# Sums over features split between the two row halves of TensorE, with an order of matmuls and banks laid out by a plan

## The chip, the cores and the metric

The kernel runs on one core of a Trainium2 chip. The metric is the device time of one execution in microseconds (us). The engines are TensorE (PE, matmuls; PEld its weight loads), VectorE (DVE), ScalarE (ACT), GpSimd (POOL) and SyncE (SP), which here issues most DMAs.

## The reference

One attention block and one gated feed-forward block read the same normalised rows; their results are multiplied and added to the input. S = 2048 rows, D = 576 features, 32 heads of 18, F = 4608 hidden features, all float32.

```python
xn = layernorm(x)
q, k, v = split_heads(xn @ wqkv)                    # 32 heads of 18
p = softmax(q @ k.T * 18 ** -0.5)
s = merge_heads(p @ v) @ wo
gate, up = xn @ W_gate, xn @ W_up                   # 576 -> 4608
h = gate * (gate > 0) * up
g = silu(h @ W_down)                                # 4608 -> 576
out = x + s * g
```

## The kernel before

Each float32 operand of a large product is split into a high part (float32r) and a remainder, and a product is the sum of three matmuls (`PRODUCTS`: high x high, high x rest, rest x high). The products of probabilities and values (`po`) are plain float32.

**Row halves.** TensorE's array is used as two tiles of 64 rows and 128 columns, which work at the same time on two different sums. D = 576 is nine chunks of 64 features (`KC`). Each tile of x holds one such chunk twice, on partitions 0 to 63 and on 64 to 127; gate weights lie on the lower half, up weights on the upper one. `row_half` gives the 27 matmuls of one sum (9 chunks x 3 products) on one half, and `row_pairs` deals them out in turn for the two halves. Maxima of scores (`pm`, reduced by DVE at L189) and scores for the exponentials (`psx`, evicted by ACT at L624) also take 64 rows each: head 0 of a pair on the lower half, head 1 on the upper one.

**Projections.** For each of four groups of 512 rows: layer norm, nine transposes (`tps`) with a split by ACT and DVE, four blocks of q and k (`pq`) with a rest block `qk_last` every second group, then v (`pv`). q, k and v go to DRAM. In the last group the first heads' k and q strips are loaded (`load_k`, `load_q`, DMAs at L147) behind block 0 of four.

**Units.** There are 144 units: 36 blocks of 128 hidden features for each 512 rows. `emit_unit` writes the order of PE by hand: 27 steps of `up` on each half (`pg`), mixed at even distances with maxima (`max_steps`, for the next pair of heads) and scores (`exp_steps`). After it `attend` multiplies the four tiles of probabilities that are ready by the values (`po`, tiles of 128 rows and 32 columns, added up in one bank `psO` over four units), and after every second unit `down` runs 48 matmuls of `py` on the whole array, then `run_tasks` does what was put off: a transpose of the maxima (`tp`, its rows written into qT by eight DMAs from `nt`, L572) and the normalisation of a finished output. The first 16 units (`N1`) have maxima only; then each of the 16 pairs of heads has 8 units (`UN`).

**Other engines.** POOL splits the gate and up weights (`gw`), the down weights (`dw`) and the hidden tile (`hh`). DVE adds `py` to the sums `ys` (L503). When 512 rows are complete, their gate value (silu) is made in small pieces between the units (`gate_steps`: exponential on ACT, reciprocals on DVE at L524) and stored in DRAM. At the end the output projection (`pw`) runs for 16 tiles of 128 rows, multiplied by the gate and added to x.

PSUM has eight banks: five shared by `pm`, `psx`, `py` and transposes, one for `po`, two for `pg`. PE's instructions keep the order of the program.

## Time and profile before

| | |
|---|---|
| median of 3 runs | 2690.13 us (2689.19 to 2692.2) |
| the profiled execution | span 2689.7 us, 0.4 us below that median; no other time of its own is given |
| mean granted TensorE clock | 0.998 |
| PE busy | 2664.5 us (99%) |
| DVE, ACT, POOL busy | 1904.3, 1386.8, 1249.1 us (71%, 52%, 46%) |
| DMA | 248.68 MB, 92 GB/s on average |

Where a row is a group, it gives line, engine, operation, output and inputs, shapes and count, then the busy time in us and the mean of one in ns, then idle time before it and what ended it. Rows of the chain or of a timeline begin with start and length in us. Busy times of overlapping matmuls are counted once for the group and in full for the mean.

### The profile page before, as it was taken

What the parts mean: (1) busy time and instruction counts of PE and PEld (TensorE: products, weight loads), DVE (VectorE), ACT (ScalarE), POOL (GpSimd) and SP (SyncE); (2) the same over time, 40 slices, a digit from 0 to 9 for tenths busy, and PEclk for the clock granted to TensorE, in tenths of its full rate; (3) what the DMA queues carried; (4) which work ended last, traced back from release to release, by engine and by line L of the source; (5) the groups of instructions that cost most, each with busy time, mean ns of one, the idle gap of its engine ahead of it and who ended that gap; (6) DMA issues with size and microseconds to landing.
All of it is one profiled execution on the core that took longest, in us unless ns stands there. A gap on an engine that the chain in (4) does not pass through costs nothing.

```text
span 2689.7 us, 55016 instructions
## 1 busy us (share of the span) xinstructions
PE 2664.5 (99%) x22092; PEld 2084.7 (78%) x22092; DVE 1904.3 (71%) x3252; ACT 1386.8 (52%) x2566; POOL 1249.1 (46%) x1021
## 2 busy tenths in 40 slices
PE   7999999999999999999999999999999999999999
PEld 6998987777777787777777777777777777777778
DVE  5426667777777777777777877777777787776135
ACT  3321125555565555555566555555555555555551
POOL 5226664444444444444444454444445444444543
PEclk9999999999999999999999999999999999999999
DMA  9745332222532322232353222222252322222237
GB/s 241 221 158 140 93 76 68 65 70 73 121 97 61 83 64 74 61 77 63 76 128 86 71 75 64 74 69 67 73 122 78 85 76 70 70 64 56 57 102 229
DMA packets 289471, 248.68 MB, mean 92 GB/s; under 512 B 60416, under 2 KB 232192, under 8 KB 289216
## 3 DMA queue, kind: packets, MB, share of 16 engines
q1 hardware_dynamic: 281152, 216.85, 32.1%
q0 software_dynamic: 8064, 28.32, 3.1%
q8 instruction: 174, 2.85, 0.5%
q14 instruction: 81, 0.66, 0.1%
HBM read 199.74 MB, written 44.83 MB: 91 GB/s over the span
## 4 chain that ended last, share of the span: by engine, by line
PE 95%; DMA 2%; DVE 1%; POOL 1%; issue 1%; SPq 1%; ACT 0%; ACTq 0%; POOLq 0%
PE pg L64 31%; PE po L64 18%; PE py L64 18%; PE pm L64 11%; PE psx L64 10%; PE pq L64 3%; PE pw L64 2%; PE pv L64 2%; PE tps L67 1%; PE tp L67 1%; SPq L147 0%; DVE e L524 0%; DMA qT<-qd 0%; DMA kT<-kd 0%; DMA rgw<-in_A_wqkv_dram 0%
## 5 line engine op out<-in xcount | busy, mean ns | idle before, releaser
L189 DVE TENSOR_REDUCE mx<-pm 128x1 f32<-128x512 f32 x2048 | 1350.6, 685 | 222.9 <-PE pm L64 85.8
L624 ACT ACTIVATE p<-psx 128x512 f32<-128x512 f32 x2048 | 1155.9, 599 | 531.6 <-PE psx L64 456.1
L64 PE MATMUL pg<-x,gw 64*128 64x512 f32 x7560 | 1388.7, 393 | 0.0
L64 PEld LDWEIGHTS pg<-x,gw 64*128 64x128 f32 x7560 | 1079.1, 186 | 85.0 <-issue 2.9
L64 PE MATMUL psx<-qT,kT 56*128 56x512 f32 x2048 | 809.1, 397 | 0.4 <-DVE mx L189 0.4
L64 PE MATMUL pm<-kT,qT 54*128 54x512 f32 x2048 | 799.9, 410 | 0.1
L64 PEld LDWEIGHTS py<-dw,hh 128*128 128x128 f32 x3456 | 460.4, 188 | 58.3 <-POOL hh L477 51.3
L64 PE MATMUL py<-dw,hh 128*128 128x288 f32 x3456 | 477.8, 297 | 0.9 <-POOL hh L477 0.8
L503 DVE TENSOR_TENSOR y<-py,y 128x288 f32<-128x288 f32 x544 | 248.6, 457 | 324.9 <-PE py L64 324.6
L64 PEld LDWEIGHTS pm<-kT,qT 54*128 54x128 f32 x2048 | 376.8, 185 | 115.3 <-issue 31.9
L64 PE MATMUL po<-p,va 128*32 128x512 f32 x4096 | 466.0, 595 | 0.0
L64 PEld LDWEIGHTS psx<-qT,kT 56*128 56x128 f32 x2048 | 378.6, 185 | 34.4 <-DVE mx L189 1.4
L98 POOL TENSOR_TENSOR gw<-rg,gw 128x1152 fp32r<-128x1152 f32 x144 | 385.7, 2679 | 11.5
L474 POOL CAST hh<-h 128x512 fp32r<-128x512 f32 x127 | 77.4, 610 | 614.1 <-DVE h L472 613.6
L97 POOL CAST dw<-rd 128x576 fp32r<-128x576 f32 x144 | 95.6, 664 | 562.7 <-PE py L64 167.5
L64 PEld LDWEIGHTS po<-p,va 128*32 128x32 f32 x4096 | 120.1, 110 | 261.7 <-issue 255.1
L98 POOL TENSOR_TENSOR dw<-rd,dw 128x576 fp32r<-128x576 f32 x144 | 205.7, 1429 | 11.6
L477 POOL TENSOR_TENSOR hh<-h,hh 128x512 fp32r<-128x512 f32 x144 | 183.8, 1277 | 24.7 <-ACT hh L476 12.5
L97 POOL CAST gw<-rg 128x1152 fp32r<-128x1152 f32 x144 | 164.9, 1145 | 0.0
L566 ACT ACTIVATE nt<-tp 32x128 fp32r<-32x128 f32 x32 | 8.5, 267 | 299.8 <-PE tp L67 299.8
L471 ACT ACTIVATE h<-pg 128x512 f32<-128x512 f32 x144 | 86.4, 600 | 134.0 <-PE pm L64 67.7
L472 DVE TENSOR_TENSOR h<-pg,h 128x512 f32<-128x512 f32 x136 | 92.6, 681 | 78.3 <-ACT h L471 78.3
(82 smaller groups left out, 1247.1 us busy)
## 6 DMA issues: line engine op xcount, KB each, us to landing
rg<-in_B_W_gate_dram SPq DMA_DIRECT2D x144, 288.0 KB
rg<-in_B_W_up_dram SPq DMA_DIRECT2D x144, 288.0 KB
rd<-in_B_W_down_dram SPq DMA_DIRECT2D x144, 288.0 KB
x<-xTd SPq DMA_DIRECT2D x54, 256.0 KB
qT<-qd SPq DMA_DIRECT2D x384, 36.0 KB
kT<-kd SPq DMA_DIRECT2D x384, 36.0 KB
qd<-hh POOLq DMA_DIRECT2D x16, 512.0 KB, 4.2
kd<-hh POOLq DMA_DIRECT2D x16, 512.0 KB, 5.7
```

The source lines that it names most:

```text
L64: return tc.keep_in_program_order(nc.tensor.matmul(*args, **kw))
L67: return tc.keep_in_program_order(nc.tensor.transpose(*args))
L97: keep(nc.gpsimd.tensor_copy(hi, raw))
L98: keep(nc.gpsimd.tensor_tensor(lo, raw, hi.bitcast(F32), ALU.subtract))
L189: nc.vector.tensor_reduce(mx[:, g % 2, h, j, c : c + 1], ps, axis=AX.X, op=ALU.max)
L471: nc.scalar.activation(h, ps[0], AF.Relu)
L472: keep(nc.vector.tensor_tensor(h, ps[1], h, ALU.mult))
L474: keep(nc.gpsimd.tensor_copy(hh[:, 0], h))
L477: keep(nc.gpsimd.tensor_tensor(hh[:, 1], h, hh[:, 0].bitcast(F32), ALU.subtract))
L503: nc.vector.tensor_tensor(ys[j][:, cs], ps, ys[j][:, cs], ALU.add)
L566: nc.scalar.activation(nt_.bitcast(F32R), ps[0:32, 0:P], AF.Copy)
L624: nc.scalar.activation(pts[kt][:, h, i, :], ps, AF.Exp, scale=SCALE)
```

## The change

x is now kept in five tiles for each 512 rows: four of 128 different features and one with the last 64 features on both halves (`KX`, `KS`). Two sums that belong together (gate and up, q and k) are a `pair` of `Part`s. A part begins on its own half (`lead`) with the four lower or upper chunks and the rest chunk, 15 matmuls, and is ended on the other half with 12, in the same bank. The down projection is done the same way, six matmuls on each half. Where nothing else says that the first half's last matmul has landed, an empty instruction on SP (`fence`) waits for it, and the second half waits for that.

`Lanes` is a planner that runs while the program is written. It keeps a time for each half, a time at which each of eight common banks comes free, and times for DVE and ACT, and gives out matmuls and banks by them; `window` mixes parts with the scores and maxima. `cycle` writes two units and the down projection of the two units before as one window; `attend` then runs once for the two units, with eight tiles of probabilities, into a bank of its own, and the two banks of an output are added by ACT and DVE. Half of the additions of `py` go by ACT and POOL (`by_pool`).

The pieces of the gate in the loop are gone: the raw sums are stored (`store_y`), and silu is made at the end, where a tile is loaded (Sigmoid on ACT, a product on POOL). The k and q strips of the first heads are loaded behind the whole q and k window of the last group.

```diff
+class Part:
+
+
+    def __init__(self, name, lead, ops, cols, steps):
+        self.name, self.lead, self.ops, self.cols, self.steps = name, lead, ops, cols, steps
+        self.at = [0, 0]
+        self.bank = self.ps = self.ended = self.after = None
+        self.out = False
+
+
+class Lanes:
+
+
+    COL, FIX, EVICT, SERVE, FENCE = 0.000446, 0.0035, 0.28, 0.08, 0.5
+
+    def __init__(self, banks, make, matmul, fence):
+        self.make, self.matmul, self.fence = make, matmul, fence
+        self.t = [0.0, 0.0]
...
+        self.free = [0.0] * banks
...
+    def take(self, now):
+        free = [(f, b) for b, f in enumerate(self.free) if not self.used[b] and f <= now]
+        if not free:
+            return None
+        b = min(free)[1]
+        self.used[b] = True
+        self.synced = max(self.synced, self.wrote[b])
+        return b
...
+    def issue(self, lane, cols):
+        self.last = max(self.t[lane], self.last)
+        self.t[lane] = self.last + cols * self.COL + self.FIX
+        self.n += 1
+        return self.t[lane]
...
+    def evict(self, bank, ps, end, steps):
+        at = end + self.EVICT
+        for server, length, fn in steps:
+            at = max(self.server[server], at) + length
+            self.server[server] = at
+            fn(ps)
+        self.free[bank] = at + self.SERVE
+        self.wrote[bank] = self.n
+        self.used[bank] = False
...
+    def ready(self, lane, p):
+        if lane == p.lead:
+            return p.bank is not None or self.spare(self.t[lane]) > 0
+        if p.after is not None and p.at[1] == len(p.ops[1]) - 1 and not p.after.out:
+            return False
+        return p.at[1] > 0 or (p.ended is not None and self.synced >= p.ended)
...
+    def step(self, lane):
+        p = self.main[lane][0]
+        w = 0 if lane == p.lead else 1
+        if p.bank is None:
+            p.bank = self.take(self.t[lane])
+            p.ps = self.make(p.bank, p.name)
+        ops = p.ops[w]
+        if w == 1 and p.at[1] == 0 and self.synced < p.ended:
+            self.fence(p.ps)
+            self.fences += 1
+            self.synced = p.ended
+        left, right = ops[p.at[w]]()
...
+        end = self.issue(lane, p.cols)
+        if done:
+            self.main[lane].popleft()
+            if w == 0:
+                p.ended = self.n
+                p.end = end
+            else:
+                self.evict(p.bank, p.ps, end, p.steps)
+                p.out = True
...
+    def fenced(self, lane, p):
+        return lane != p.lead and p.at[1] == 0 and p.ended is not None and p.end + self.FENCE <= self.t[lane]
...
+    def score(self, lane, scores):
+        m, x = scores[lane]
+        pick = m if m and (not x or self.server["V"] <= self.server["A"] or len(m) > len(x) + 3) else x
+        if m and x and len(x) > len(m) + 3:
...
+            order = (0, 1) if self.t[0] <= self.t[1] else (1, 0)
+            lane = next((l for l in order if self.main[l] or waiting(l)), None)
+            if lane is None:
+                break
+            main = bool(self.main[lane]) and self.ready(lane, self.main[lane][0])
+            other = waiting(lane) > 0 and self.room(lane)
+            if main and not (credit[lane] >= 1 and other):
+                cols = self.main[lane][0].cols
+                credit[lane] = min(credit[lane] + waiting(lane) * cols / max(1, left[lane]), 3.0)
+                left[lane] -= cols
+                done += cols
+                self.step(lane)
+            elif other:
+                credit[lane] = max(credit[lane] - 1, -3.0)
+                done += 512
+                self.score(lane, scores)
+            elif self.main[lane] and self.fenced(lane, self.main[lane][0]):
+                left[lane] -= self.main[lane][0].cols
+                done += self.main[lane][0].cols
+                self.step(lane)
+            else:
+                stuck += 1
...
-    psS = ctx.enter_context(tc.tile_pool(name="psS", bufs=5, space=PSUM))
-    psO = ctx.enter_context(tc.tile_pool(name="psO", bufs=1, space=PSUM))
-    psG = ctx.enter_context(tc.tile_pool(name="psG", bufs=2, space=PSUM))
+    banks = ctx.enter_context(tc.tile_pool(name="banks", bufs=1, space=PSUM))
...
+    def fence(ps):
+        nc.sync.clobber_nop(outs=[nc.sync.lower_ap(ps)])
+
+    lanes = Lanes(8, bank, mm, fence)
...
+    def pair(names, xt, ops, cols, steps):
+
+        parts = []
+        for o in range(2):
+            def lane_ops(lane, o=o):
+                places = [(4 * o + i, i) for i in range(KX - 1)]
+                if lane == o:
+                    places.append((KS - 1, KX - 1))
+                rows = lane_rows(lane)
+                return [
+                    (lambda s=s, i=i, a=a, b=b: ops(rows, s, a, xt[o][i][rows, b, :]))
+                    for s, i in places
+                    for a, b in PRODUCTS
+                ]
+
+            parts.append(Part(names[o], o, [lane_ops(o), lane_ops(1 - o)], cols, steps[o]))
+        return parts
+
+    def in_turn(pairs):
+
+        return [[p[l] for p in pairs] + [p[1 - l] for p in pairs] for l in range(2)]
...
-            for b in range(4):
-                if b == 0 and g == 0:
...
-                if b == 0 and g == NQ - 1:
-                    load_q(0, 0)
-                    for c in range(NQ):
-                        load_k(0, c)
...
+            pairs = [qk_pair(b, wqk[b], g) for b in range(4)]
+            first = pairs[:2] + ([qk_last(wqk[4], g - 1)] if g % 2 else [])
+            parts = [a + b for a, b in zip(in_turn(first), in_turn(pairs[2:]))]
+            spread = [0.1 + 0.85 * i / 12 for i in range(12)]
+            ins = stepped(fill, spread)
+            lanes.window(parts, None, ins)
...
+                load_q(0, 0)
+                for c in range(NQ):
+                    load_k(0, c)
+                load_q(0, 1)
+                up_weights(0)
+                pms = [maxima(0, h) for h in range(2)]
+            vp = v_pairs(wv, g)
+            va_, vb_ = in_turn(vp[:2]), in_turn(vp[2:])
+            scores = None
+            if g == NQ - 1:
+                scores = [(deque(pms[h].popleft() for _ in range(NP)), deque()) for h in range(2)]
+            lanes.window([a + b for a, b in zip(va_, vb_)], scores)
...
+        gate, up_ = pair(
+            ("pg", "pu"), (xcur[g], xcur[g]), lambda rows, s, a, xr: (gw[rows, a, s, :], xr),
+            512, [[("A", 0.6, relu)], [("V", 0.69, times)]],
+        )
+        up_.after = gate
+        return [gate, up_]
...
+        def by_pool(ps):
+            t = hp.tile([P, HC], F32, name="yt")
+            nc.scalar.activation(t, ps[:, :HC], AF.Copy)
+            keep(nc.gpsimd.tensor_tensor(ys[j][:, cs], t, ys[j][:, cs], ALU.add))
...
+        return [("A", 0.41, by_pool)] if side else [("V", 0.46, add)]
...
+                def lane_ops(lane, cs=cs, js=js):
+                    rows = lane_rows(lane)
+                    return [
+                        (lambda hh=hh, w=w, a=a, b=b: (hh[rows, a, js], w[rows, b, cs]))
+                        for hh, w in terms
+                        for a, b in PRODUCTS
+                    ]
+
+                parts.append(Part("py", n, [lane_ops(n), lane_ops(1 - n)], HC, add_up(j, n, f, n)))
...
-    def gate_steps():
-
-        while gates:
-            y, t = gates.pop(0)
-            e = wl.tile([P, D], F32, name="e", bufs=1)
-            keep(nc.scalar.activation(e, y, AF.Exp, scale=-1.0))
-            yield
-            keep(nc.scalar.activation(e, e, AF.Copy, bias=1.0))
-            for n in range(6):
-                yield
-                cs = slice(n * GP, (n + 1) * GP)
-                tc.keep_in_program_order(nc.vector.reciprocal(e[:, cs], e[:, cs]))
-            keep(nc.gpsimd.tensor_tensor(y, y, e, ALU.mult))
-            nc.gpsimd.dma_start(gd[t * P : (t + 1) * P, :], y)
-            yield
...
+    def store_y(k):
+        g, f = units[k]
+        if f == NF - 1:
+            for j in range(4):
+                t = g * 4 + j
+                nc.sync.dma_start(yd[t * P : (t + 1) * P, :], ys[j])
...
-    def attend():
-
-        va, qp, kt, p, done = ready.pop(0)
-        if kt == 0:
-            po[0] = psO.tile([P, 512], F32, name="po")
-        for i in range(2):
...
+    def attend(u, qp, done):
+
+        va = vas[u % 2]
+        b, ps = lanes.hold("po")
+        batch = sorted(ready, key=lambda r: r[0])
...
+        end = lanes.pause(len(batch) * 0.86 + 0.3)
...
+        lanes.evict(b, ps, end, [("V", 0.69, add)] if ots else [("A", 0.6, copy)])
...
-        while ready:
-            attend()
-        if k % 2 == 0 and k:
-            for _ in down(k - 1):
-                pass
-            run_tasks()
...
+    def cycle(k, scores):
+
+        up_weights(k + 1)
+        ups = []
+        ins = []
+        downs = down(k - 1) if k else []
+        down_weights(k)
+        if k > N1:
+            groups = [downs[:2], [up(k), downs[2]], [up(k + 1), downs[3]]]
+        elif k:
+            groups = [[up(k), downs[0]], downs[1:3], [up(k + 1), downs[3]]]
+        else:
+            groups = [[up(0), up(1)]]
+        order = [in_turn(g) for g in groups]
+        parts = [[p for o in order for p in o[l]] for l in range(2)]
+        turn_over = units[k + 1][1] == NF - 1 and k + 2 < len(units)
+        ins.append((0.65, lambda: (gus.pop(k), up_weights(k + 2))))
+
+        if turn_over:
+            ins.append((0.8, lambda: load_x(units[k + 2][0], 0)))
+        lanes.window(parts, scores, ins)
+        gus.pop(k + 1)
+        down_weights(k + 1)
+        if k:
+            store_y(k - 1)
+        if turn_over:
+            del xcur[units[k][0]]
+            for c in range(1, KX):
+                load_x(units[k + 2][0], c)
...
+            scores = [
+                (deque(pms[h].popleft() for _ in range(min(16, len(pms[h])))), exps(u, h, qp, range(k0, k0 + NT // 2)))
+                for h in range(2)
+            ]
+            now = tasks[:] if i % 2 == 0 else []
+            cycle(N1 + UN * u + 2 * i, scores)
...
+            attend(u, qp, done)
+            run_tasks(now)
+            del tasks[: len(now)]
...
+        sg = f2.tile([P, D], F32, name="sg", bufs=2)
+        nc.scalar.activation(sg, gt, AF.Sigmoid)
+        nc.gpsimd.tensor_tensor(gt, gt, sg, ALU.mult)
```

700 lines of the change are left out of this document (363 added, 337 removed).

## Prediction

> **What bounds the kernel now.** I read the page first: busy time of each engine and the chain that ended last.
>
> ```profile
> span 2689.7 us, 55016 instructions
> PE 2664.5 (99%) x22092; PEld 2084.7 (78%) x22092; DVE 1904.3 (71%) x3252; ACT 1386.8 (52%) x2566; POOL 1249.1 (46%) x1021
> PE 95%; DMA 2%; DVE 1%; POOL 1%; issue 1%; SPq 1%; ACT 0%; ACTq 0%; POOLq 0%
> ```
>
> TensorE is busy all the time and is 95% of the chain, so a change counts by what it does to PE's own queue: matmuls taken out, matmuls brought closer together, or a new wait in front of one. Next the groups by line tell what PE does.
>
> ```profile
> L64 PE MATMUL pg<-x,gw 64*128 64x512 f32 x7560 | 1388.7, 393 | 0.0
> L64 PE MATMUL psx<-qT,kT 56*128 56x512 f32 x2048 | 809.1, 397 | 0.4 <-DVE mx L189 0.4
> L64 PE MATMUL py<-dw,hh 128*128 128x288 f32 x3456 | 477.8, 297 | 0.9 <-POOL hh L477 0.8
> ```
>
> The loop uses three shapes of the array: 64x128 tiles on two row halves (pg, psx, and pm like psx), the whole array (py), and, in the weight loads shown below, 128x32 tiles (po). Busy times overlap within a pair of halves and hide the pace. The chain of waits in order of time shows it where one kind runs alone, and it shows the period of the loop by the starts of py.
>
> ```profile
> 122.86 14.70 PE pq L64 x126
> 153.71 14.29 PE pv L64 x216
> 1368.15 3.57 PE po L64 x32
> 393.89 6.56 PE py L64 x48
> 1128.80 6.56 PE py L64 x48
> 1163.23 6.56 PE py L64 x48
> 1198.34 6.56 PE py L64 x48
> 2459.83 6.56 PE py L64 x48
> ```
>
> 126 matmuls of 512 columns are 63 pairs: 14.70 / 63 = 0.233 us a pair. 216 of 288 columns are 108 pairs: 14.29 / 108 = 0.132 us. The full-array py does 48 in 6.56 us, 0.137 each with its edges. One cycle of the loop is two units and one down projection; neighbouring py starts are 34.43 us apart (1128.80 to 1163.23) or 35.11 (to 1198.34, with the transposes of the tasks). From 393.89 to 2459.83 I count 59 cycles: 35.02 us on average, so about 0.25 us more than the 34.77 mean of a quiet pair of cycles.
>
> Inside a cycle, the timeline of PE and of its weight loads:
>
> ```profile
> 1357.72 0.50 PE L64 MATMUL pg<-x,gw 64*128 64x512 f32 x1
> 1358.06 0.39 PE L64 MATMUL psx<-qT,kT 56*128 56x512 f32 x1
> 1368.08 3.64 PE L64 MATMUL po<-p,va 128*32 128x512 f32 x32
> 1370.25 0.13 PEld L64 LDWEIGHTS po<-p,va 128*32 128x32 f32 x4 [0.30 <-issue]
> 1370.68 0.13 PEld L64 LDWEIGHTS po<-p,va 128*32 128x32 f32 x4 [0.30 <-issue]
> ```
>
> A round of four po matmuls takes 0.43 us (1370.25 to 1370.68), so a section of 8 rounds should take 3.44 and takes 3.57: 0.13 at its end. A unit's section runs 1357.72 to 1368.08, 10.36 us; its 86 matmuls are 43 pairs, 10.02. The 0.34 left is at the edges: the second pair starts 0.34 after the first instead of 0.23, and the rest lies before po.
>
> **The sum of a cycle before.** 86 pairs x 0.233 = 20.04; 16 rounds of po x 0.43 = 6.88; py 48 x 0.132 = 6.34 (the pv pace); together 33.26 of 34.43. The other 1.17 are changes of the array's shape and small stalls: 2 x 0.34 + 2 x 0.13 + about 0.2 around py.
>
> **The change on PE.** The number of matmuls of 64 rows for gate, up, q, k and v stays: an output took 27 on one half, and takes 15 on one and 12 on the other. So "summing over both halves" is worth nothing by itself. The down projection becomes 96 matmuls of 64 rows in place of 48 of 128, 48 pairs at 0.132: 6.34 again. What goes is the switching: the cycle has one window of paired matmuls and one po section, so 0.34 + 0.13 = 0.47 in place of 1.17, a gain of 0.70 a cycle. [...]
>
> The gate leaves the loop. Its reciprocals sit among the maxima on DVE:
>
> ```profile
> L189 DVE TENSOR_REDUCE mx<-pm 128x1 f32<-128x512 f32 x128 | 82.8, 680 | 17.5 <-PE pm L64 11.4 <-PE pg L64 3.7 <-PE psx L64 0.8
> L524 DVE RECIPROCAL e<-e 128x96 f32<-128x96 f32 x12 | 8.9, 742 | 0.0
> L503 DVE TENSOR_TENSOR y<-py,y 128x288 f32<-128x288 f32 x23 | 10.5, 457 | 14.7 <-PE py L64 14.7
> ```
>
> I put the 0.25 us a cycle above the quiet mean down to them and to the turn-overs of x, and let them go. Loop: 59 x 0.25 + 64 x 0.70 = 15 + 45 = 60 us gained, before new waits.
>
> **New waits in the loop.** The rows are POOL's groups, two bursts of SP's queue, and the longest wait of SP in total.
>
> ```profile
> L474 POOL CAST hh<-h 128x512 fp32r<-128x512 f32 x127 | 77.4, 610 | 614.1 <-DVE h L472 613.6
> L477 POOL TENSOR_TENSOR hh<-h,hh 128x512 fp32r<-128x512 f32 x144 | 183.8, 1277 | 24.7 <-ACT hh L476 12.5
> L97 POOL CAST dw<-rd 128x576 fp32r<-128x576 f32 x144 | 95.6, 664 | 562.7 <-PE py L64 167.5
> L98 POOL TENSOR_TENSOR dw<-rd,dw 128x576 fp32r<-128x576 f32 x144 | 205.7, 1429 | 11.6
> 1450.08 5.03 SPq L572 DMA_DIRECT2D qT<-nt  x8
> 1462.64 2.10 SPq L147 DMA_DIRECT2D kT<-kd  x6
> SPq L133 <- POOL gw L98: 847.1, 128, 13.1
> ```
>
> Four places, with their cover. (1) Window and DVE: 32 maxima x 0.65 (82.8 / 128) + 4 additions x 0.46 + 2 products of 512 columns, priced like a maximum at 0.68, = 24 us of DVE in a window of 26.4 + edges. With the banks it can drain into the po section, so it is covered, but closely; each stall is paid by an in-order PE. (2) The halves of py have half their additions taken by ACT and POOL. (3) POOL prepares hh (0.61 + 1.28) and dw (0.66 + 1.43) after the window's end, about 5 us with an addition of 288 columns (half of 1.43). The po section covers it, now 6.88 long; without that cover it would be 5 us a cycle. (4) The fence: the second half of a sum may not start before the first has landed, so an empty instruction on SP waits for one half and releases the other. If SP is idle it costs nothing, because the plan puts at least 0.5 us between them. If SP issues DMAs, PE waits behind them.
>
> Bounds of all four together: 0 when all are covered, to 2.5 us a cycle, which is half of the 5.03 us burst. It cannot be a gain, since the 33.26 is already at pace. I take 0.5 us, nearer to the low end, since the plan spaces fences and the stalls PE shows today are that small (0.0 to 0.9 in the groups): 64 x 0.5 = 32 us lost.
>
> **The sixteen units before the loop.** Their cycles have no po, so nothing covers POOL's 5 us of hh and dw:
>
> ```profile
> 302.96 6.57 PE py L64 x48
> 323.53 6.55 PE py L64 x48
> ```
>
> A cycle is 20.57 us, of which about 60.5 pairs x 0.233 + 6.34 = 20.44 is pace: nothing to win. The plan puts 3.5 us of pg (15 x 0.233) ahead of the first py, so about 1 us of the 5 stays open: 8 x 1 = 8 us lost (0 to 16).
>
> **Projections.** Nine transposed tiles for each 512 rows become five. Rows of the chain, of SP and of PE:
>
> ```profile
> 14.75 1.81 PE pq L64 x11
> 54.56 16.73 PE pv L64 x202
> 174.93 16.28 SPq L147 DMA_DIRECT2D kT<-kd  x24
> 199.03 1.51 PE L64 MATMUL pv<-wv,x 64*128 64x288 f32 x18
> ```
>
> The first q and k matmuls begin at 14.75 and the first v block at 54.56, 39.8 later, for 108 pairs x 0.233 = 25.2 us of matmuls: the rest is transposed tiles, at 0.55 (a row below), and waits for them. After the change five tiles are ready before the first matmul, which I estimate at 16, and five of the next rows lie in the window: 16 + 25.2 + 2.8 = 44, so 10 us sooner. Sixteen tiles fewer in all; the later groups gain about 6 more. Against it stands a moved step: the loads of kT and qT of the first heads were issued behind the first block of the last group, 25 us ahead of the v block that uses them; now they are issued behind the whole window. 24 strips took SP 16.28 us, the plan spreads the maxima evenly over v, and the fourth needs the last strip. PE waits about 12 us (0 to 16). Net -4 us.
>
> **The end.** Reciprocals of the last gates stand in the chain of the tail:
>
> ```profile
> 2612.56 1.82 PE pw L64 x14
> 2626.11 2.53 DVE e L524 x4
> 2652.80 0.55 PE tps L67 x5
> 2653.35 3.71 PE pw L64 x28
> 2685.78 0.47 DVE gt L792
> ```
>
> A tile at pace is 4.26 us; the sixteen take 2612 to 2686, 74 for 68. The sigmoid goes to ACT and its product to POOL, beside the sum that is there: two of 576 columns, 1.43 + 1.43 by the row of dw, under 4.26. I take -5 us (-8 to +6, since wo and the gate now load only after buffers come free).
>
> **Sum.** 2689.7 - 60 + 32 + 8 - 4 - 5 = 2661 on the profile's span; the median 2690.13 is 0.4 above it and moves nothing. As PE pace alone, without new waits in loop and units, it is 2621. I say 2660; this case's own range is 2615 to 2684.
>
> **Rivals.** Beside that forecast (chance 0.52):
>
> The window becomes a DVE window (chance 0.18). For it: 24 of 26.4 us, and eight banks of which up to four hold unfinished sums. Against it: in the row of L189, four cycles, DVE stood 17.5 us waiting for PE, 4.4 a cycle. PE would then lose about 0.95 us a cycle, as much as it gains in switches and gate, and the time is 2661 + 64 x 0.45 = 2690; from 2675 to 2705. [...]
>
> Fences stuck behind SP (chance 0.26), the one that ends slower. Place: the two boundaries per unit of heads at which the eight qT<-nt transfers are issued, just where the window's first sums change halves. They take 5.03 us, the first change comes about 2.5 us into the window, so PE waits 2.5 us, and with six strips issued behind them (2.10) 4.6. 32 x 2.5 = 80 us: 2741; with the strips 147: 2808. It decides from 0.95 us a cycle on, the 0.5 and another 0.45. For it: SP already stands 847 us behind POOL. Against it: those waits are ahead of need, and SP's order need not follow the program's text.
>
> That the edit does nothing, since the switches stay (chance 0.04): if every fence drains both halves, the 0.47 comes back several times in a cycle, 2690 to 2720.
>
> **How the numbers follow.** Differences under 0.2% (5.4 us) can't be told from no change. Faster: the forecast's 0.52 and half of the DVE rival, 0.09: 0.61. Same: 0.05 of the middle of that rival. Slower: the rest of it 0.04, fences 0.26, switches 0.04: 0.34. The range reaches from 2610 (all new waits covered: 2621, and the tail and the first wait at their best) to 2765, above the first price of the fence rival; about 0.1 lies beyond, with the dearest fences, and 0.1 below or in sums I mis-sized.
>
> **What would show it.** Right: a cycle of two units near 34.6 us on average (34.1 without new waits), po in sections of 64 matmuls with one edge each, py pairs 0.132 apart, no L524, the first pv near 44, pm stalled near the first maxima. Wrong: PE idle with SP as the releaser behind qT<-nt, PE weight loads of pm waiting for DVE mx throughout the window, py waiting for POOL dw at a window's start, or 64-row py pairs slower than 0.132.

## The result and the profile after

The changed kernel takes 3512.14 us (median of 4 runs, 3504.81 to 3521.36) beside 2691.16 us of the kernel before on the same chip: ratio 1.3054, 95% interval 1.3027 to 1.3082. The forecast was 2660 us. It was wrong, and not in its sign alone: the loss is 821 us, where the dearest case that it priced was 147 us above the forecast.

The page of the changed kernel, in the same places as before: the span, the busy times, the granted clock in 40 slices, the chain by engine, and three of PE's groups.

```profile
span 3503.0 us, 62995 instructions
PE 2891.1 (83%) x25436; PEld 2250.0 (64%) x25436; DVE 1739.0 (50%) x2888; ACT 1479.6 (42%) x2755; POOL 1438.8 (41%) x1273
PEclk9988889989998988999899998999999999999889
PE 44%; POOL 25%; SPq 15%; issue 9%; DVE 4%; DMA 2%; ACT 1%; POOLq 0%; DVEq 0%; ACTq 0%
L239 PE MATMUL pg<-x,gw 64*128 64x512 f32 x3888 | 1271.7, 430 | 168.2 <-SPq L260 160.2
L239 PE MATMUL pu<-x,gw 64*128 64x512 f32 x3888 | 1270.7, 429 | 56.0 <-SPq L260 54.9
L239 PE MATMUL py<-dw,hh 64*128 64x288 f32 x6864 | 745.2, 321 | 347.1 <-SPq L260 340.7
```

Two things have changed. PE is idle for 612 us (3503.0 - 2891.1), and it is busy for longer, 2891 us where it was 2664, though the matmuls that are new are halves of old ones. The chain has 25% of POOL and 15% of SP's queue in it, where PE had 95% before. The group rows name the releaser: SP at L260, which is the empty instruction of `fence`, called the marker from here on.

The waits of PE (line, releaser and its line, us in total, times, longest):

```profile
PE py L239 <- SPq L260: 340.7, 64, 8.9
PE pg L239 <- SPq L260: 160.2, 63, 5.8
PE pu L239 <- SPq L260: 54.9, 14, 5.7
PE pq L239 <- SPq L260: 10.3, 2, 9.3
```

And the waits of SP's own queue:

```profile
SPq L318 <- POOL gw L275: 837.8, 142, 13.0
SPq L622 <- POOL dw L275: 445.9, 74, 12.9
```

With two of `pv` (5.7 us) these are 145 waits of PE for the marker, 572 us in all. SP itself stands behind POOL: the loads of the next weights (L318, L622) write into a buffer that POOL is still reading to make `gw` or `dw`, and the marker is queued behind those loads. Both sides of one such place, first SP's timeline, then POOL's and PE's:

```profile
1460.14 5.02 SPq L755 DMA_DIRECT2D qT<-nt  x8
1531.53 0.39 SPq L318 DMA_DIRECT2D rg<-in_B_W_gate_dram  x1
1533.16 0.51 SPq L321 DMA_DIRECT2D rg<-in_B_W_up_dram  x1
1528.83 2.67 POOL L275 TENSOR_TENSOR gw<-rg,gw 128x1152 fp32r<-128x1152 f32 x1
1465.83 1.80 PE L239 MATMUL py<-dw,hh 64*128 64x288 f32 x12 [7.71 <-SPq L260]
1533.79 0.49 PE L239 MATMUL pg<-x,gw 64*128 64x512 f32 x1 [2.44 <-SPq L260]
```

POOL's subtraction ends at 1531.50; at 1531.53 SP can issue the first load, after four of them, at 1533.67, it comes to the marker, and PE, idle since 1531.35, goes on at 1533.79. The first row is the place that the prediction named: the eight writes qT<-nt, 5.02 us, ahead of a marker, and PE waits 7.71 us. Going through the visible waits between 300 and 3400 us by what SP had issued last, 31 of them lie behind these writes and the store `od<-ob` after them (243.6 us, 7.9 each), 72 behind loads of gate and up weights (188 us, 2.6 each), 19 behind loads of down weights (59 us), 15 behind strips of qT (49 us).

The rest is PE's own pace. The stretches ahead of, inside and behind a slow part that follows the second of these waits, by the view of windows (start:end, length, busy times, granted clock, DMA):

```profile
1533.80:1534.60 0.80, 0.80 (x7) 0.69 (x9) 0.00 (x0) 0.00 (x0) 0.00 (x0) 1.00 0.46 117
1534.60:1538.00 3.40, 3.40 (x20) 2.86 (x18) 1.38 (x2) 1.39 (x3) 0.00 (x0) 0.50 0.23 69
1538.20:1541.00 2.80, 2.80 (x33) 2.09 (x33) 2.30 (x4) 2.06 (x5) 0.17 (x1) 1.00 0.18 56
```

0.8 us after PE restarts, the granted clock falls to 0.50 for 3.4 us, and its multiplications of 512 columns come 0.43 us apart instead of 0.233 (1535.40, 1535.83, 1536.25, 1536.68 in PE's timeline). Between 300 and 3400 us the records of the clock hold 125 such stretches, each 3.413 us long or two or three times that, 628 us in all.

### The profile page after: what moved, and what is told of

Its sections match the earlier page's. It is cut to its first block, busy times and chain, and to the rows that moved or that the text cites. A ratio compares the mean times of both kernels' runs of the same rounds, so it can differ in the third digit from the quotient of the medians.

```text
span 3503.0 us, 62995 instructions
## 1 busy us (share of the span) xinstructions
PE 2891.1 (83%) x25436; PEld 2250.0 (64%) x25436; DVE 1739.0 (50%) x2888; ACT 1479.6 (42%) x2755; POOL 1438.8 (41%) x1273
## 4 chain that ended last, share of the span: by engine, by line
PE 44%; POOL 25%; SPq 15%; issue 9%; DVE 4%; DMA 2%; ACT 1%; POOLq 0%; DVEq 0%; ACTq 0%
PE pg L239 12%; POOL gw L275 11%; PE pu L239 9%; PE py L239 7%; PE psx L239 5%; PE pm L239 5%; POOL gw L274 4%; SPq L755 4%; SPq L321 4%; SPq L318 4%; POOL y L673 3%; PE pq L239 3%; DVE h L643 3%; POOL hh L649 3%; POOL hh L646 2%
## 5 line engine op out<-in xcount | busy, mean ns | idle before, releaser
L239 PE MATMUL pg<-x,gw 64*128 64x512 f32 x3888 | 1271.7, 430 | 168.2 <-SPq L260 160.2
L239 PE MATMUL pu<-x,gw 64*128 64x512 f32 x3888 | 1270.7, 429 | 56.0 <-SPq L260 54.9
L239 PE MATMUL py<-dw,hh 64*128 64x288 f32 x6864 | 745.2, 321 | 347.1 <-SPq L260 340.7
L239 PEld LDWEIGHTS pg<-x,gw 64*128 64x128 f32 x3888 | 790.7, 209 | 291.2 <-SPq L260 181.9
L239 PEld LDWEIGHTS py<-dw,hh 64*128 64x128 f32 x6864 | 686.6, 209 | 430.1 <-SPq L260 361.7
L239 PEld LDWEIGHTS pu<-x,gw 64*128 64x128 f32 x3888 | 796.0, 208 | 108.4 <-SPq L260 60.1
L673 POOL TENSOR_TENSOR y<-yt,y 128x288 f32<-128x288 f32 x268 | 215.6, 805 | 452.3 <-ACT yt L672 451.9
L275 POOL TENSOR_TENSOR gw<-rg,gw 128x1152 fp32r<-128x1152 f32 x144 | 383.1, 2661 | 11.6
L668 DVE TENSOR_TENSOR y<-py,y 128x288 f32<-128x288 f32 x268 | 121.0, 452 | 398.9 <-PE py L239 398.6
L672 ACT ACTIVATE yt<-py 128x288 f32<-128x288 f32 x268 | 111.0, 414 | 400.1 <-PE py L239 391.4
L643 DVE TENSOR_TENSOR h<-pu,h 128x512 f32<-128x512 f32 x144 | 99.0, 687 | 162.8 <-ACT h L639 140.7
```

The costliest lines, as they stand in the source:

```text
L239: return keep(nc.tensor.matmul(*args, **kw))
L275: keep(nc.gpsimd.tensor_tensor(lo, raw, hi.bitcast(F32), ALU.subtract))
L643: keep(nc.vector.tensor_tensor(h, ps, h, ALU.mult))
L673: keep(nc.gpsimd.tensor_tensor(ys[j][:, cs], t, ys[j][:, cs], ALU.add))
```

## The experiments

Differences are against the kernel before in the same series of runs (2691.63, 2690.30, 2691.96 or 2692.87 us).

**The marker on another engine.** The empty instruction is issued by ACT (e2) or DVE (e3) instead of SP; nothing else differs.

```diff
-        nc.sync.clobber_nop(outs=[nc.sync.lower_ap(ps)])
+        nc.vector.clobber_nop(outs=[nc.vector.lower_ap(ps)])
```

> The changed kernel with the fence's empty instruction on ACT in place of SP; nothing else. ACT's queue holds no weight loads. Theory A: PE's waits for fences fall from 572 us to under 60, PE stays busy, the granted clock returns to about 1.0, PE busy falls from 2891 to about 2600 us, and the time comes near the sum on record, 2640 to 2720. Rival B (a fence costs about 2 us on any engine): about 3500 us. Rival C: waits go but PE busy stays near 2890, so about 2930 us.

> The changed kernel with the fence's empty instruction on DVE in place of SP. Theory A: as with ACT, waits under 60 us in all, 2640 to 2740 us; DVE's queue is denser than ACT's, so up to 40 us more than on ACT. Rival B: about 3500 us. Rival C: about 2930 us.

On ACT 2679.12 us (ratio 0.9953, 0.9936 to 0.9969), on DVE 2678.46 us (0.9953, 0.9937 to 0.9969). Rivals B and C fall. With one word changed, 834 us are gone and the kernel is 13.2 us faster than before. The page of the version on DVE:

```profile
PE 2628.6 (98%) x25436; PEld 2079.6 (78%) x25436; DVE 1735.2 (65%) x2888; ACT 1472.1 (55%) x2755; POOL 1441.3 (54%) x1273
```

The largest waits of its PE, and one of its weight loads:

```profile
PE tps L242 <- DVE xn L443: 19.8, 8, 10.5
PE py L239 <- POOL dw L275: 5.2, 5, 1.1
PE pm L239 <- DMA kT<-kd: 2.5, 1, 2.5
PEld pg L239 <- DVE h L643: 25.7, 56, 0.5
```

Two of its sections of `po`, on the chain:

```profile
420.32 7.00 PE po L239 x64
2464.78 7.00 PE po L239 x64
```

Of the waits for the marker 0.2 us is left, and PE's busy time is 262 us shorter than on SP. The spans of the two profiles differ by 826 us: 564 of idle time (other waits grew by 8) and 262 of busy time. On SP, PE was busy for 507 us at half clock, on DVE for 11. A stretch of 3.41 us at half clock costs four tiles of `po` 1.70 us in c4, below (5.34 for 3.64), so I estimate half of the difference, 248 us, for the clock: nearly all of the 262. 59 cycles lie between the two `po` rows: 34.65 us each, against 35.02 before.

**The weights' buffers doubled.** If SP stands behind POOL because there is one buffer of raw weights, a second one should let it run ahead (paid for by one buffer fewer of `h`).

```diff
-    wr = pool(early, "wr", 1)
+    wr = pool(early, "wr", 2)
...
-            made.append(hp.tile([P, 512], F32, name="h"))
+            made.append(hp.tile([P, 512], F32, name="h", bufs=1))
```

> The changed kernel with two raw weight buffers (rg) in place of one; to make room, one buffer for h in place of two. Theory A (fences stand behind SP's weight loads, which wait until POOL has split the buffer before): a load no longer waits for the split just before it, so much of the 572 us in which PE waits for SP goes; I expect 150 to 300 us of such waits, a clock nearer to 0.95 and 2900 to 3150 us. Rival B (each of the 290 fences costs PE about 2 us by itself, wherever SP stands): waits stay near 570 us and the time near 3510. Rival C (the 64-row matmuls of unequal length are slow by themselves): PE busy stays near 2890 us in either case.

3517.11 us, ratio 1.307 (1.3043 to 1.3096): nothing gained, and my expectation of 2900 to 3150 fell. The waits of SP, then of PE, are as they were:

```profile
SPq L318 <- POOL gw L275: 737.3, 111, 12.9
SPq L622 <- POOL dw L275: 547.1, 136, 12.8
```

```profile
PE py L239 <- SPq L260: 351.1, 63, 9.1
```

The time is the one that rival B gave, but B is excluded by the runs above. As I read SP's order, a load is still placed about where its buffer comes free, only for a later block, and there it waits for POOL as before, 1284 us in the two rows as in the changed kernel. More depth moved the loads in the queue and did not take the wait out of it.

**The loads on another queue.** The marker stays on SP, and POOL issues the loads of weights itself.

```diff
-                nc.sync.dma_start(
+                eng.dma_start(
...
-        load9(rg, [[(wg, f * P, P)], [(wu, f * P, P)]])
+        load9(rg, [[(wg, f * P, P)], [(wu, f * P, P)]], nc.gpsimd)
...
-        nc.sync.dma_start(rd, wd[f * P : (f + 1) * P, :])
+        nc.gpsimd.dma_start(rd, wd[f * P : (f + 1) * P, :])
```

> The changed kernel with its fences on SP as written, but the loads of gate, up and down weights (rg, rd) issued by POOL in place of SP. If what held the fences were these loads' waits for POOL's splits, then SP is free for them: PE's waits for SP fall from 572 us to under 100, the clock returns to 0.98 or more, and the time to 2680 to 2800 us (POOL pays about 0.6 us for each of some 700 issues, 5 to 7 us a cycle, and may come late with hh and dw). If SP's other work held them (strips of q and k, the eight qT writes, which stay), the waits stay over 300 us and the time over 3100 us.

2894.78 us, ratio 1.0761 (1.0742 to 1.0781), granted clock 0.972. The waits of its PE:

```profile
PE py L239 <- SPq L260: 88.4, 30, 3.3
PE py L239 <- POOL dw L275: 33.2, 17, 5.0
PE pq L239 <- SPq L260: 13.5, 2, 12.9
```

The waits of `pg` and `pu` for the marker are gone. What remains of them is two places per pair of heads, behind qT<-nt: 30 waits of 2.95 us, 88.4 us. That is the place of the prediction's rival, and its price, 32 x 2.5 = 80. So the loads were the larger part, and they also made the waits behind qT<-nt longer, 7.9 us each instead of 2.95, by bringing SP to these writes late: in the changed kernel the first of the eight starts 4.6 us after ACT has made `nt` (mean of 32), here 0.03. The expectation (2680 to 2800 us, waits under 100, a clock of 0.98) was too good: all waits for the marker are 109 us, and against the version on DVE the profile has 142 us more of idle time and 72 more of busy time at the lower clock. Part of that is the price of the edit itself, since POOL, which now issues the loads, comes later with `dw` (33.2 us for 5.2).

**One marker on SP in the kernel before.** Nothing of the change but one such marker in each of the 72 down projections, after three of the six matmuls of its first sum.

```diff
+                    if i == 3 and j == 0 and n == 0:
+                        nc.sync.clobber_nop(outs=[nc.sync.lower_ap(ps)])
```

> The kernel before with one fence on SP in each down projection (72 in all): in its first sum, after three of six matmuls, PE waits for SP, which waits for those three. Theory A: SP stands behind a weight load that waits for POOL in about half the cycles there too, though with two buffers; 72 fences cost about 1 to 3 us each, 70 to 220 us, and after the long ones the clock falls: 2760 to 2950 us. Rival B (about 2 us a fence without any queue): 2830 us, with all fences equally long. If fences are cheap unless a load stands before them, the waits are of very unequal length.

2746.01 us, ratio 1.0204 (1.0184 to 1.0225), 54 us more. Its PE waits for the marker:

```profile
PE py L64 <- SPq L500: 32.1, 71, 6.9
```

0.45 us on average, 6.9 at most, and a clock of 0.996: one marker per cycle costs 0.76 us a cycle, more than the 0.5 that I took for all of them; the changed kernel has 3.2 per cycle in its loop. (Here it waits for matmuls issued just before it; the plan puts at least 0.5 us between.) The waits are of unequal length, as expected for a queue, but the 54 us lie below the 70 to 220 that I expected.

**Does idle time alone slow the clock?** Into the version with the marker on DVE a gap is put on purpose: after the fourth of the eight tiles of a `po` section, DVE copies the bank so many times, and then issues an empty instruction for which the fifth waits. One copy (c1), two (c3), four (c4); c2 has one copy and four DVE operations on a tile of its own.

```diff
+            if n == 3:
+                for _ in range(4):
+                    keep(nc.vector.tensor_copy(idle, ps))
+                nc.vector.clobber_nop(outs=[nc.vector.lower_ap(ps)])
```

> The version with the marker on VectorE, with a gap put into TensorE's queue on purpose: after the fourth of the eight key tiles of each of the 72 or so value sums, DVE copies the bank (which waits for the products so far) and then issues the empty instruction that the next product waits for; about 1 us of idle TensorE each. Theory A (an idle time as short as this leaves the pace alone): 64 to 72 gaps of 0.9 to 1.3 us, pairs of multiplications 0.233 apart right behind them, 2678 + 60 to 95, granted clock 0.99 or more. Theory B (each break of the queue costs pace, whatever its length): pairs of 0.42 behind each, another 1 to 2.5 us each, 2678 + 130 to 270, granted clock near 0.95.

> The same gap made longer: four DVE operations of 512 columns stand between the copy and the empty instruction, about 3 us of idle TensorE at the same place. Theory A (the pace falls behind idle times of 2 us and more): besides 64 to 72 gaps of 2.8 to 3.8 us (180 to 270 us) the pairs behind each are 0.42 apart for some 2 to 3 us, which costs another 1 to 1.4 us each (65 to 100 us): 2678 + 250 to 370, granted clock 0.95 to 0.97. Theory B (the slow pace of the changed kernel has another cause than the idle time): gaps alone, 2678 + 180 to 270, pairs of 0.233 right behind them, granted clock 0.99 or more.

> As the run with the 1-us gap, with two DVE copies of the bank ahead of the empty instruction instead of one: TensorE idle 1.6 us in each of 64 places (0.9 with one copy, and 0.69 more). Theory A (the pace falls behind an idle time of about 2 us): hardly any slow pace yet, 2747 + 64 x 0.69 = 2791, up to 2825 if a third of the gaps are followed by 2 us of slow pace; granted clock 0.98 or more. Theory B (the slow pace of the changed kernel has another cause): 2791, no pairs of 0.42 at all.

> With four copies: idle 3.0 us in each of 64 places. Theory A: 64 x 3 x 0.69 = 132 us of idle more than with one copy, and behind nearly each gap some 2 to 3 us at 0.42 instead of 0.233 a pair, that is 1 to 1.4 us lost: 2747 + 132 + 64 to 90 = 2943 to 2969; TensorE's busy time larger by 64 to 90; granted clock about 0.97. Theory B: 2879, TensorE's busy time as with one copy (2642), clock 0.99 or more.

2747.21, 2873.32, 2799.40 and 2947.22 us. c2 did not do what I meant: its four operations do not touch the bank, the marker went ahead of them, and the gap stayed 0.9 us. It has another use, below. For c1, then c3, then c4: the engines' line of the page, and the waits of PE for the marker; for c4 two rows of PE's timeline besides.

```profile
PE 2642.3 (96%) x25436; PEld 2077.4 (76%) x25436; DVE 1778.9 (65%) x2952; ACT 1472.9 (54%) x2755; POOL 1442.1 (53%) x1273
```

```profile
PE po L239 <- DVEq L830: 54.9, 64, 0.9
```

```profile
PE 2641.9 (94%) x25436; PEld 2071.3 (74%) x25436; DVE 1824.3 (65%) x3016; ACT 1473.9 (53%) x2755; POOL 1441.2 (52%) x1273
```

```profile
PE po L239 <- DVEq L829: 108.6, 64, 1.7
```

```profile
PE 2698.6 (92%) x25436; PEld 2079.4 (71%) x25436; DVE 1911.9 (65%) x3144; ACT 1472.5 (50%) x2755; POOL 1438.1 (49%) x1273
```

```profile
PE po L239 <- DVEq L829: 201.8, 64, 3.5
```

```profile
506.63 5.34 PE L239 MATMUL po<-p,va 128*32 128x512 f32 x32 [3.15 <-DVEq L829]
546.66 3.64 PE L239 MATMUL po<-p,va 128*32 128x512 f32 x32 [3.15 <-DVEq L829]
```

Gaps of 0.9 and of 1.7 us have the same busy time of PE (2642.3 and 2641.9, beside 2628.6 without them) and a clock of 0.997. Gaps of 3.15 us make it 57 us longer at a clock of 0.976, with 34 stretches of half clock after 300 us where c1 and c3 have one. So idle time alone is enough, and theory B falls. But A's "behind nearly each gap" was wrong too: of the 64 sections 31 run the four tiles behind the gap in 3.64 us, and 33 take longer, 21 of them 5.34, as the two rows show. The total lay in the range of A all the same, partly by luck: more idle time than expected (3.15 us a gap for 3.0) and less slow pace (57 us for 64 to 90). What tells the sections apart is when they restart: taken modulo 3.4133 us, the length of one slow stretch, from the start of the span, the restarts of all fast ones fall between 0.48 and 1.39, and those of the slow ones outside. In the changed kernel, above, a gap of 2.44 us cost the clock as well: 0.50 for 3.4 us.

The traces also show what such a gap has to do. The slow stretches of one run begin on a grid of 3.4133 us, within 4 ns. Two periods of that grid at each of the two rows, with PE's busy time alone (start:end, length, busy time, granted clock, DMA):

```profile
504.54:507.95 3.41, 1.32 (x14) 1.00 0.29 87
507.95:511.36 3.41, 3.41 (x22) 0.50 0.21 58
542.07:545.49 3.42, 1.45 (x16) 1.00 0.10 32
545.49:548.90 3.41, 2.23 (x24) 1.00 0.32 91
```

The first gap leaves 2.09 us of one period idle, and the next period runs at half clock. The second gap is as long but is split over two periods, 1.97 and 1.18 us, and the clock stays. So it goes for all periods that begin at full clock after 300 us: in c4 the limit lies at 2.03 to 2.04 us of idle time in a period (33 of 737 are followed by half clock). In the changed kernel it lies between 1.78 and 1.79 (125 of 752), and in c3, where no period has more than 1.70, none is. Short gaps in one period add up: two of 0.93 and 0.92 us, in the changed kernel's period from 322.88 us, were enough. Why the limit differs between runs stays open.

**The parts of the change, with the marker on DVE.** In e4 the down projection stays on the whole array, as a section of its own; in e7 the values are multiplied after each unit again, with the window cut in two; b3 is the kernel before with only the gate moved to the end.

```diff
+        if k > N1:
+            down_whole(k - 1)
...
-            groups = [downs[:2], [up(k), downs[2]], [up(k + 1), downs[3]]]
+            groups = [[up(k)], [up(k + 1)]]
```

```diff
+            one_ = [[p for o in order[:2] for p in o[l]] for l in range(2)]
+            lanes.window(one_, scores)
+            second[0]()
+            ins[0][1]()
...
+            lanes.window(order[2], second[1](), ins)
```

```diff
-                    gates.append((ys[j], g * 4 + j))
+                    t_ = g * 4 + j
+                    nc.sync.dma_start(gd[t_ * P : (t_ + 1) * P, :], ys[j])
...
+        sg = f2.tile([P, D], F32, name="sg", bufs=2)
+        nc.scalar.activation(sg, gt, AF.Sigmoid)
+        nc.gpsimd.tensor_tensor(gt, gt, sg, ALU.mult)
```

> The changed kernel with its fences on DVE, and in 63 of the 64 cycles of the loop the down projection undone: 48 matmuls of 128 rows in a section of their own ahead of the window, additions as in the change. By the sum on record the section brings back its switches: about 0.13 behind po, 0.2 behind py, so 0.3 to 0.5 us a cycle, 20 to 30 us over the version with all sums on lanes (2678): about 2700. The rival (64-row matmuls of 288 columns among those of 512 cost something in the window, whose 27.3 us are 0.95 above pace) says that the window falls to pace and the time stays at 2660 to 2680.

> The changed kernel with its fences on DVE, and values multiplied after each unit again: in 63 of the 64 cycles of the loop the window is cut in two with four tiles of probabilities each, a copy or an addition more per cycle. By the sum on record a second po section costs its two switches, 0.34 + 0.13 = 0.47 us, and the end of a second window, 0.2 to 0.4: 0.7 to 0.9 us a cycle, 44 to 57 us over 2678: 2720 to 2735. If the merging of the sections gained nothing, the time stays within 2670 to 2690.

> The kernel before with one part of the change alone: the gate's pieces taken out of the loop, raw sums stored, silu made where a tile is loaded at the end (Sigmoid on ACT, product on POOL). I put the 0.25 us a cycle above the quiet pair of cycles to the reciprocals and the turn-overs of x, 15 us, and 5 us in the tail: 2670 to 2680 us. If the turn-overs alone made the 0.25, only the tail gains: 2685.

2692.03 us (ratio 1.0008, 0.9998 to 1.0017), 2699.54 (1.0034, 1.0022 to 1.0045) and 2677.16 (0.995, 0.9935 to 0.9965). Set against the 13.2 us that the version on DVE gains on the kernel before, undoing the down projection costs 15 us, undoing the common section of values 22, and the gate alone brings 13.1, as much as the whole change with its marker moved. The first two cost less than expected (20 to 30 and 44 to 57 us). For e7 the wait of PE, then two starts on the chain of b3:

```profile
PE py L239 <- POOL dw L275: 23.9, 36, 1.1
```

```profile
394.27 6.55 PE py L64 x48
2445.06 6.55 PE py L64 x48
```

Of e7's 22 us, 23.9 - 5.2 = 19 are waits for POOL's `dw`, which the longer `po` section covers. The other 3 are not the price of the second section: e7 also lacks a stall of the version on DVE, `pg` behind `h`, that is worth 14 us (next experiment). The section's edges can be read from the starts of the matmuls (medians between 450 and 2400 us). It starts 0.22 us after the last `py` (0.13 at pace), what follows starts 0.52 after its last round (0.43 at pace), and the pair of `pg` behind that 0.34 later (0.23 at pace): 0.28 us a cycle, 18 us in all, and 19 + 18 - 14 = 23. In b3 the mean of 59 cycles is 34.76 us; by the spans 15.1 us are gained in the loop and 0.1 behind it, where 5 were expected.

**The plan's mistake.** With the marker on DVE one regular stall was left, the `PEld` row shown with it: a weight load of `pg` waits for DVE's `h`, 0.46 us once per cycle. The plan gives the bank of `up` back when DVE could have made the product, and does not know that the product waits for ScalarE's relu before it. One entry of no length on ScalarE tells it so (e8). e9 adds to it that ScalarE copies the 64 columns that both row halves hold twice.

```diff
-            512, [[("A", 0.6, relu)], [("V", 0.69, times)]],
+            512, [[("A", 0.6, relu)], [("A", 0.0, lambda ps: None), ("V", 0.69, times)]],
```

```diff
-                nc.vector.tensor_scalar(
-                    xn[:, j, D:], xt[:, j, C4:], mv[:, j, 0:1], rs[:, j : j + 1], op0=ALU.subtract, op1=ALU.mult
-                )
+                nc.scalar.activation(xn[:, j, D:], xn[:, j, C4:D], AF.Copy)
```

> The version with the marker on VectorE, and one line more in the plan's list of evictions: the product of the second bank of a feature block is put down as waiting for ScalarE's relu before it. In the version without this line the first weight load of pg waits once per cycle for DVE's h, 25.7 us over 56 waits (0.46 each), because the plan believes the bank free sooner than it is. Theory A (the order believes a bank free too early, and nothing else is in the way): that wait goes and nothing takes its place; 0.3 to 0.4 us a cycle, so 2678 - 64 x 0.35, about 2656 (2650 to 2665). Theory B (the banks are short, not the belief): the plan puts the start elsewhere and another bank's start waits instead; within 5 us of 2678.

> The one with the corrected plan, and the 64 columns that both row halves hold twice are written by a ScalarE copy of the normalised columns instead of a second DVE subtraction and multiplication. In the version with the marker on VectorE one such DVE operation of 64 columns took 0.31 us alone and 2.61 us while POOL ran its 2.65 us subtraction of the weights. Theory A (it is these operations that made the start some 2 to 3 us later): first pq 2 to 4 us sooner, total 2 to 4 us under the one with the corrected plan alone. Theory B (DVE's longer operation of 576 columns meets POOL's work anyway): start within 1 us, total within 2 us.

2664.62 us (ratio 0.9901, 0.9884 to 0.9917) and 2661.01 us (0.9888, 0.9873 to 0.9903): 27.3 and 31.0 us below the kernel before, and the fastest of all. Two sections of `po` in e8's timeline of PE, 58 cycles apart, and the weight load that waits now:

```profile
422.22 7.07 PE L239 MATMUL po<-p,va 128*32 128x512 f32 x64
2417.62 7.07 PE L239 MATMUL po<-p,va 128*32 128x512 f32 x64
```

```profile
PEld pm L239 <- DVE h L643: 14.1, 56, 0.3
```

A cycle takes 34.40 us, 0.25 less than without the entry, not 0.3 to 0.4, since `pm` waits for the same `h` in place of `pg`, though for half as long: theory A, in part. In e9 the first matmul of q comes at 17.56 instead of 20.90 (21.05 in e8). The 3.6 us between the medians of e8 and e9 fit that, but their runs overlap (2664.1 to 2667.5 and 2659.8 to 2665.4 us), so the total alone shows nothing.

## Why the prediction was wrong, point by point

**The step that failed** is the fourth of the new waits, the price of the marker. The prediction named the mechanism ("if SP issues DMAs, PE waits behind them"), and its rival the place. Then it took 0.5 us a cycle for all four new waits, bounded them by half of one burst of writes, 2.5 us, and set the likeliest case where "the plan spaces fences". Measured are 834 us, or 13.0 for each of 64 cycles if all is put there: 8.9 of waits and 4.1 of longer busy time, nearly all of it halved clock. Three things were missing. The plan keeps times for two row halves, the banks, DVE and ACT; it keeps none for SP, so its spacing of 0.5 us says nothing of SP. The 847 us in which SP stood behind POOL were quoted and then set aside as "ahead of need": they were ahead of need for the data, but in the changed kernel the marker stood behind such waits in SP's queue, 1284 us of them, and PE waited 572 us for it in all. And idle time was priced as itself, where here 1.8 us of it within one period of 3.41 us also cost the clock.

**The rival of the fences** (0.26) had the right sign and place. With the loads away its price of the waits held, 88.4 against 80. For the changed kernel it was ten times too small. Of the 754 us that it lacks, 164 are longer waits at its own places (243.6 for 80), 262 longer busy time, and the other 328 mostly markers behind loads of weights and strips of qT, places that it did not name.

**The other new waits** were sized well. With the marker on DVE, PE waits 5.2 us for `dw` over the whole program, and the plan's mistake is worth 14. The DVE rival did not come about either. c2 tells how near it was: 380 us more of DVE's work than in c1 (2158.6 against 1778.9), 5.9 us a cycle, made PE wait for DVE (52.3 us of `pm` behind `ot`, 18.5 behind `ob`) and cost 126 us, 2.0 a cycle, some of it at a clock of 0.990. So DVE seems to have had some 4 us of room in a cycle; this is an estimate, since c2 adds its work in the `po` section and not in the window.

**The gate**, 0.25 us a cycle, was right: b3 has the 34.76 that the quiet cycles showed (34.77). The turn-overs of x, to which the prediction gave a share, are unchanged in b3, so the gate's pieces made all of it.

**The switches**, 0.70 a cycle, were about right, though whole cycles hide it. Read like the edges of e7, b3 has two `po` sections a cycle with 0.39 and 0.36 us of edges and 0.20 behind `py`, 0.95 in all; e8 has one section with 0.28, that is 0.67 less. By whole cycles b3 to e8 gains 0.36, and b3 to the version on DVE 0.11, where the sum had 0.70 - 0.50 = 0.20 after the new waits. What lies between is lost inside the window: 0.25 a cycle is the plan's mistake, and the other 0.31 was not followed. The down projection's switch, about 0.2 in the sum, is 15 / 63 = 0.24 in e4. The average cycle of 34.6 us that was to show the forecast right is 34.65 in the version on DVE.

**Projections** (-4 forecast): the first v matmul was to come 10 us sooner, at 44, and came 1.7 later. Rows of the timeline of the version on DVE, first DVE, then POOL and PE:

```profile
10.26 0.31 DVE L446 TENSOR_SCALAR xn<-xt,mv,ln 128x64 f32<-128x64 f32 x1
10.97 2.61 DVE L446 TENSOR_SCALAR xn<-xt,mv,ln 128x64 f32<-128x64 f32 x1
13.51 2.91 DVE L443 TENSOR_SCALAR xn<-xt,mv,ln 128x576 f32<-128x576 f32 x1
10.75 5.35 POOL L404 TENSOR_TENSOR wqk<-rgw,wqk 128x1152 fp32r<-128x1152 f32 x2 [7.69 <-ACT wqk L403]
20.90 4.48 PE L239 MATMUL pq<-x,wqk 64*128 64x512 f32 x36
56.30 0.40 PE L239 MATMUL pv<-wv,x 64*128 64x288 f32 x1
```

The first q matmul starts at 20.90, not at 16: fewer transposes did not help while the rows to be transposed came late (the 19.8 us of `tps` behind `xn` among the waits). The wait for the strips of kT, 12 us in the sum, measured 2.5. In sum the first matmul of the feature units starts at 218.6 against 218.1: nothing gained.

**The sixteen units** (+8): in the version on DVE the multiplications of the first 16 units end 12.9 us later than before, those of the first 20 units 8.4 later, in orders that have done slightly different other work by then. The forecast's own range of 0 to 16 holds both.

**The end** (-5): from the first output projection to the end e8 takes 74.4 us (2588.85 to 2663.2, on the chain) against 77.1: -2.7.

Without the marker's price the version on DVE gains 13 us: 22.7 in the loop from the 20th unit to the last and 4.0 at the end, against 8.4 lost by the 20th unit and 5.3 at the hand-over from the loop to the end, where one `po` section of 64 matmuls (7.07 us) stands in place of one of 32 (3.57). The 29 of the forecast need the plan's mistake mended, too. That e9's 2661 lies by the forecast of 2660 is therefore no confirmation of it.

## What to carry to other kernels

An empty instruction that orders two engines waited here for what stood ahead of it on the engine that issued it: 572 us of PE's waits with it on SP, 0.2 us on DVE. Before placing one, read that queue's own waits in the profile (here 847 us behind POOL), and put it on an engine whose queue is short and moves with the consumer. A planner's spacing counts only for the resources that it models. Where TensorE is the bound, price a new wait at its length and, by c1 and c3, some 0.2 us more: their 64 gaps of 0.9 and 1.7 us, 54.9 and 108.6 us of waits, cost 69 and 121 us over the version on DVE, at the same clock of 0.997. Where the waits left 1.79 us (the changed kernel) or 2.04 us (c4) of one 3.41-us period idle, the next period ran at half clock; in c4 that cost 57 us over 33 sections, 1.7 us each.

## What the runs showed of the hardware that I had not expected

The granted clock fell to one half for 3.41 us behind gaps of 2.44 us (the changed kernel) and 3.15 us (c4). In these two runs the idle time of TensorE within one period of a grid of 3.4133 us told which periods were followed by half clock: the limit was 2.03 to 2.04 us in c4, between 1.78 and 1.79 in the changed kernel. Gaps of one and the same length, 3.15 us in c4, so cost the clock in 33 sections and not in 31.

In the version on DVE, DVE's operation of 64 columns took 2.61 us instead of 0.31, and the one of 576 columns behind it 2.91 instead of 0.58, while POOL ran two subtractions: the first of these two ends within 0.04 us of POOL's first, the other 0.3 us after POOL's second. In e9 the 64-column operations are on ScalarE and one such meeting is left (2.87 us for 576 columns), and q started 3.3 us sooner; so both theories of that run hold in part.
